# Forgetting attention with a SiLU MoE on one core: transposes of two batches moved ahead, and MoE pieces spread evenly between the steps

## The chip, the core and the metric

The kernel runs on one core of a Trainium2 chip. The metric is the device time of one execution in microseconds, taken as the median over several runs. The five engines are written as in the profile: PE is TensorE (matmuls; PEld are its weight loads), ACT is ScalarE, DVE is VectorE, POOL is GpSimd, and SP is the queue from which most transfers are started.

## The reference

Attention with a forget gate over 8 batches of 8 heads, 576 rows and head width 64, and after it a two-layer MoE with a SiLU in between, on the 4608 rows of all batches:

```python
scores = scale * q @ k.T                     # 8 x 8 x 576 x 576
decay = cum[:, None] - cum[None, :]          # cum = cumsum(log f)
attn = softmax(where(causal, scores + decay, -1e9))
x = (attn @ v).transpose(0, 2, 1, 3).reshape(4608, 512)
h = x @ w_in                                 # 512 -> 2048
out = (h * sigmoid(h)) @ w_out               # 2048 -> 512
```

The decay is folded into the values: they, and a column of ones beside them, are multiplied by exp(-cum) (`w_bf`), so a softmax is an exponential, a mask, a matmul and a division by the last column.

## The kernel before, in words

**The attention, first blocks.** Of each batch the first 128 rows are a block that can be done alone. For one batch b there are these steps on TensorE, with their lines in the profile:

- `turn0(b)`: q and k of the block are transposed by 32 small matmuls (L271) into two tiles `tp`; q's is copied into a tile `qkT` by ACT, k's into `kT0[b]` by DVE (L278).
- `ban0(b)` (batches 0 to 3 only): two matmuls (L286) put the causal mask into a tile `sc`.
- `scores0(b)`: eight matmuls (L305) into `sc`; ACT takes the exponential into `u` (L312). For batches 4 to 7 `mask0(b)` multiplies `u` by the triangle on DVE (L321).
- `out0(b)`: eight matmuls of `u` and the values (L340) into a tile that takes a buffer of the same kind as `sc`; DVE makes the reciprocal (L348) and the product `xq` (L350).
- `back0(b, copy)`: four transposes of `xq` (L362), and a copy into the MoE's input by ACT or DVE (L364).

Batches 0 to 3 are done by an order written out by hand, before any MoE work is possible. Batches 4 and 5, then 6 and 7, are done by `two_more(b)`, with MoE work between the steps.

**The rest of the attention.** A loop over 16 values of m takes two pairs of heads per turn: `scores` (L433, exponentials L437 and L449), `attend` (L478 and L487, with L495 and L496 on DVE) and, a turn later, `back` (L508). Between them stand calls of `slot`, which fill in MoE work.

**The MoE.** The rows are in ten groups: one of 512 tokens (the blocks of batches 0 to 3), two of 256 (batches 4 and 5, batches 6 and 7), and later ones of 384 and 256. Its work is cut into pieces of four matmuls on TensorE. An m1 piece (`m1_chunk`, L532) makes one `hp` tile of the first product; ACT takes the tanh (L540) and DVE makes `gt` of it (L541). An m2 piece (`m2_part`, L570) adds a quarter of the second product into a tile `po`; after the fourth, ACT copies it out (L579) and it is stored.

**Who decides the order.** Every engine works through its queue in the order in which the program is written. `step()` writes the next piece, m1 or m2. When both can be done it compares how far each is in its group; if the two fractions are less than 0.3 apart it takes the kind that wasn't taken last, else the one that is behind. `fill(us, first)` calls `step()` until pieces worth `us` have been written, by an estimate of their length; what was written too much is kept in `at["left"]` and deducted from the next call, so a call may write no piece. `first` names the kind to begin with.

**Buffers.** PSUM is used up by two tiles of the kind `sc` (scores, and the products of `out0`) and four of the kind `big` (`tp`, `hp`, `po`, `tx`, and the products of `attend`). The tiles `qkT` have three buffers; from batch 4 on, two of them are taken by the transposed q and k of the loop's first two turns, so that the two batches of a `two_more` share the third.

Of the kernel before, what the change touches and what calls it, by code (L numbers as in the profile page):

```python
# [18 lines left out]
def kernel(  # L19
# [110 lines left out]
    def load_v0(b):  # L130
        t = vfs[b % 4]
        nc.sync.dma_start(out=t[:, :, 0:D], in_=v[b, :, 0:P, :].rearrange("h p d -> p h d"))
        vf0[b] = t
# [85 lines left out]
    def keep_warm(n):  # L219
        t = pbig.tile([P, SM], FP32, name="wm", tag="big")  # L220
        for _ in range(n):
            nc.tensor.matmul(t[:, :], lhsT=warm[:, 0:P], rhs=warm[:, :], start=True, stop=True)  # L222
# [37 lines left out]
    def turn0(b, between=0):  # L260
        src = qk0.pop(b)
        qT0[b] = qktp.tile([P, NP, P], BF16, name="qkT", tag="qkT")
        for i, (dst, evac) in enumerate(
            ((qT0[b], nc.scalar.copy), (kT0[b], nc.vector.tensor_copy))
        ):
            if i == 1 and between:
                keep_warm(between)
            tp = pbig.tile([P, NP, NRUN, RUN], FP32, name="tp", tag="big")
            for c in range(RUN):
                for j in range(2):  # L270
                    nc.tensor.matmul(  # L271
                        tp[j * D : (j + 1) * D, :, :, c].rearrange("p a r -> p (a r)"),
                        lhsT=src[:, i, c * D : (c + 1) * D],
                        rhs=sel[:, j, :],
                        start=True,
                        stop=True,
                    )
            evac(  # L278
                out=dst[:, :, :].rearrange("p a t -> p (a t)"),
                in_=tp[:, :, :, :].rearrange("p a r c -> p (a r c)"),  # L280
            )

    def ban0(b):
        sc = psc.tile([P, 2, NP, P], FP32, name="sc", tag="sc")
        for i in range(2):
            nc.tensor.matmul(  # L286
                sc[:, i, :, :].rearrange("p a t -> p (a t)"),
                lhsT=ident_bf[:, :],
                rhs=ban[:, :, :].rearrange("p a t -> p (a t)"),
                start=True,  # L290
                stop=False,
            )
        return sc

    def scores0(b, sc=None):
        t = qT0.pop(b)
        fresh = sc is None
        u = upool.tile([P, 2, NP, P], BF16, name="u", tag="u")
        u0[b] = u
        if fresh:  # L300
            sc = psc.tile([P, 2, NP, P], FP32, name="sc", tag="sc")
        for p in range(NP):
            for i in range(2):
                r = slice(i * D, (i + 1) * D)
                nc.tensor.matmul(  # L305
                    sc[:, i, p, :],
                    lhsT=kT0[b][r, p, :],
                    rhs=t[r, p, :],
                    start=fresh,
                    stop=fresh or p == NP - 1,  # L310
                )
        nc.scalar.activation(  # L312
            out=u[:, :, :, :].rearrange("p i a t -> p (i a t)"),
            in_=sc[:, :, :, :].rearrange("p i a t -> p (i a t)"),
            func=ACT.Exp,
            scale=scale,
        )

    def mask0(b):
        x = u0[b][:, :, :, :].rearrange("p i a t -> p (i a) t")  # L320
        nc.vector.tensor_tensor(  # L321
            out=x, in0=x, in1=tri[:, None, :].to_broadcast([P, H, P]), op=ALU.mult
        )
# [11 lines left out]
    def out0(b):  # L335
        dn = psc.tile([P, 2, 4, P], FP32, name="dn0", tag="sc")
        u = u0.pop(b)
        for h in range(H):
            p, i = h // 4 * 2 + h % 2, h // 2 % 2
            nc.tensor.matmul(  # L340
                dn[:, h // 4, h % 4, 0 : D + 1],
                lhsT=u[:, i, p, :],
                rhs=v0[b][:, h, :],
                start=True,
                stop=True,
            )
        rec = recp.tile([P, 2, 4], FP32, name="rec0", tag="rec0")
        nc.vector.reciprocal(out=rec[:, :, :], in_=dn[:, :, :, D])  # L348
        xq = xqp.tile([P, H, D], BF16, name="xq", tag="xq")
        nc.vector.tensor_tensor(  # L350
            out=xq[:, :, :].rearrange("p (g j) d -> p g j d", g=2),
            in0=dn[:, :, :, 0:D],
            in1=rec[:, :, :, None].to_broadcast([P, 2, 4, D]),
            op=ALU.mult,
        )
        xqs[b] = xq

    def back0(b, copy):
        xq = xqs.pop(b)[:, :, :].rearrange("p (c j) d -> p c (j d)", j=2)
        tx = pbig.tile([P, NCC, P], BF16, name="tx", tag="big")  # L360
        for cc in range(NCC):
            nc.tensor.transpose(tx[:, cc, :], xq[:, cc, :], ident_bf[:, :])  # L362
        g, c0 = HEADS_OF[b]
        copy(out=xg(g)[:, :, c0 : c0 + P], in_=tx[:, :, :])  # L364
# [160 lines left out]
    def m1_chunk(g, fc):  # L525
        w = GW[g]
        if fc == 0:
            gts[g] = gpool.tile([P, NFC, w], BF16, name="gt", tag="gt")
        gt = gts[g]
        hp = pbig.tile([P, w], FP32, name="hp", tag="big")  # L530
        for cc in range(NCC):
            nc.tensor.matmul(  # L532
                hp[:, :],
                lhsT=w_in_bf[:, cc, fc * P : (fc + 1) * P],
                rhs=xg(g)[:, cc, :],
                start=(cc == 0),
                stop=(cc == NCC - 1),
            )
        th = tpool.tile([P, w], BF16, name="th", tag="th")
        nc.scalar.activation(out=th[:, :], in_=hp[:, :], func=ACT.Tanh, scale=0.5)  # L540
        nc.vector.scalar_tensor_tensor(  # L541
            out=gt[:, fc, :],
            in0=th[:, :],
            scalar=1.0,
            in1=hp[:, :],
            op0=ALU.add,
            op1=ALU.mult,
        )
# [43 lines left out]
        else:  # L592
            M2 += [(g, tb, part) for tb in range(nt) for part in range(4)]
    M2_OF = [sum(1 for x in M2 if x[0] == g) for g in range(NG)]
    at = {"m1": 0, "m2": 0, "left": 0.0, "last": 0}
    ready: set[int] = set()
    open2 = {"w": False}

    def step():

        a, c = at["m1"], at["m2"]
        can1 = a < len(M1) and M1[a][0] in ready
        g1 = M1[a][0] if a < len(M1) else NG
        g2 = M2[c][0] if c < len(M2) else NG
        if can1 and M1[a][1] == 0 and g1 > g2 + 1:
            can1 = False
        can2 = open2["w"] and c < len(M2) and g2 < g1
        if not can1 and not can2:
            return None
        if can1 and can2:  # L610
            f1 = M1[a][1] / NFC
            f2 = (c - sum(M2_OF[:g2])) / M2_OF[g2]
            can1 = at["last"] == 2 if abs(f1 - f2) < 0.3 else f1 < f2
        at["last"] = 1 if can1 else 2
        if can1:
            m1_chunk(*M1[a])
            at["m1"] += 1
            return 4 * (GW[g1] / 2.4 + 2.5)
        m2_part(*M2[c])
        at["m2"] += 1  # L620
        return 4 * (DM / 2.4 + 2.5)
# [3 lines left out]
        t += sum(4 * (DM / 2.4 + 2.5) for g, _, _ in M2[at["m2"] :] if g in ready)  # L625
        return t / 1000

    def fill(us_, first=0):
        if first:
            at["last"] = 3 - first  # L630
        at["left"] += us_ * 1000
        while at["left"] > 0:
            t = step()
            if t is None:
                at["left"] = 0.0
                return False
            at["left"] -= t
        return True


# [17 lines left out]
    turn0(1)  # L658
    sc = ban0(0)
    scores0(0, sc)  # L660
    sc = ban0(1)
    scores0(1, sc)
    convert_v0(1)
    load_w_in(1)
    load_v0(4)
    turn0(2)
    out0(0)
    sc = ban0(2)
    scores0(2, sc)
    convert_v0(2)  # L670
    load_v0(5)
    turn0(3)
    out0(1)
    back0(0, on_dve)
    sc = ban0(3)
# [49 lines left out]

    def two_more(b):
        turn0(b)
        fill(0.6)
        turn0(b + 1)
        fill(0.6)  # L730
        scores0(b)
        mask0(b)
        fill(0.6, 2)
        scores0(b + 1)
        mask0(b + 1)
        fill(2.0, 2)
        out0(b)
        fill(0.6)
        out0(b + 1)
        fill(1.2)  # L740
        back0(b, on_act)
        fill(0.6)
        back0(b + 1, on_act)
        fill(0.6)

    fill(4.0)
    two_more(4)
    ready.add(1)
    fill(6.0)
    open2["w"] = True  # L750
    fill(5.0, 2)
    two_more(6)
    ready.add(2)
    fill(1.0, 2)
# [56 lines left out]
    while step() is not None:  # L811
        pass
# [31 lines left out]
```

The softmax here doesn't subtract the row's maximum and nothing guards it: scores larger than these inputs give would overflow.

## Time and profile before

| what | value |
|---|---|
| time, median of 3 runs | 355.41 us (355.34 to 355.89) |
| span of the profiled run | 353.1 us |
| TensorE, VectorE, ScalarE, GpSimd busy | 341.9, 188.0, 218.1, 103.4 us |
| first m1 piece starts | 19.84 us |
| first blocks of batches 4 and 5 | 24.2 to 36.4 us |
| first blocks of batches 6 and 7 | 48.5 to 60.2 us |
| the loop over m starts | 62.0 us |
| last `back` ends, MoE alone from there | 291 us |

Times within the profile are counted from the start of the span. In the timelines below each line has the start, the length, engine, source line, operation, output and input tiles, their sizes and how many instructions were joined; in brackets stands how long the engine was idle just before and what it waited for. Matmuls overlap each other and their ends are modelled, so what a group of them costs TensorE is read from its start to the start of the next group.

### The profile page before, as it was taken

Reading aid. Unit: us, or ns where it says so; the run is one execution under the profiler, and the core shown is the slowest. Engines: PE = TensorE matmul, PEld = TensorE weight load, DVE = VectorE, ACT = ScalarE, POOL = GpSimd, SP = SyncE. Lnnn points to the kernel's source line nnn. Section 1 sums busy time; section 2 is a strip of 40 time slices with the busy share of each in tenths; the row PEclk is TensorE's granted clock in tenths of the full one; section 3 lists DMA queues with packets and bytes.
Section 4 is the critical chain, followed back from the end, with each engine's and each line's share of the span. In section 5 each row is a group of like instructions: output and inputs, shape, how many; then the busy total and the mean of one; then the engine's idle time right before and its main releaser. Section 6 shows DMA issues by size and latency. Waiting matters only on the chain.

```text
span 353.1 us, 9039 instructions
## 1 busy us (share of the span) xinstructions
PE 341.9 (97%) x3646; PEld 205.0 (58%) x3646; DVE 188.0 (53%) x409; ACT 218.1 (62%) x399; POOL 103.4 (29%) x183
## 2 busy tenths in 40 slices
PE   8998999999899999999999999999999999999995
PEld 4644555667656556566565666656566565555664
DVE  4566834355657466555646654645655554535340
ACT  5646716866676756758758675676946744545341
POOL 6993146254072162145117214312600000000000
PEclk9999999999999999999999999999999999999999
DMA  8999998998885895696489594748822000010012
GB/s 161 221 203 200 200 196 177 214 220 171 191 167 126 178 183 97 147 212 151 113 174 211 116 201 106 174 103 165 170 58 58 32 32 30 30 59 33 32 60 59
DMA packets 138969, 47.92 MB, mean 136 GB/s; under 512 B 127984, under 2 KB 134384, under 8 KB 138928
## 3 DMA queue, kind: packets, MB, share of 16 engines
q1 hardware_dynamic: 132240, 40.93, 53.5%
q0 software_dynamic: 6528, 6.29, 10.8%
q8 instruction: 28, 0.46, 0.6%
q10 hardware_dynamic: 160, 0.13, 0.1%
q14 instruction: 13, 0.11, 0.1%
HBM read 36.85 MB, written 9.44 MB: 131 GB/s over the span
## 4 chain that ended last, share of the span: by engine, by line
PE 88%; ACT 4%; DVE 4%; issue 2%; ACTq 0%
PE po L570 35%; PE hp L532 32%; PE sc L433 7%; PE dn L478 5%; PE dn L487 3%; PE tp L271 2%; PE tx L508 2%; DVE gt L541 2%; PE wm L222 1%; DVE xq L350 1%; ACT th L540 1%; ACT u L437 1%; ACT osb L579 1%; ACT u L312 1%; ACT qkT L278 1%
## 5 line engine op out<-in xcount | busy, mean ns | idle before, releaser
L532 PE MATMUL hp<-x,w_in_bf 128*128 128x384 bf16 (+2 forms) x832 | 148.4, 314 | 3.3 <-DVE gt L541 2.3
L540 ACT ACTIVATE th<-hp 128x384 bf16<-128x384 f32 (+2 forms) x208 | 95.7, 475 | 88.8 <-PE hp L532 86.4
L541 DVE SCALAR_TENSOR_TENSOR gt<-th,hp 128x384 bf16<-128x384 bf16 (+2 forms) x208 | 106.1, 522 | 82.8 <-ACT th L540 79.4
L570 PE MATMUL po<-w_out_bf,gt 128*128 128x512 bf16 (+1 forms) x592 | 145.7, 374 | 0.0
L532 PEld LDWEIGHTS <-w_in_bf 128*128 128x128 bf16 x832 | 78.1, 98 | 58.5 <-issue 5.5
L570 PEld LDWEIGHTS <-gt 128*128 128x128 bf16 x592 | 55.4, 98 | 49.1 <-issue 1.7
L437 ACT ACTIVATE u<-sc 128x1024 bf16<-128x1024 f32 (+1 forms) x96 | 74.6, 814 | 12.1 <-PE sc L433 11.9
L387 POOL TENSOR_TENSOR vp<-vf,w_bf 128x520 bf16<-128x520 f32 (+1 forms) x32 | 35.7, 1118 | 44.9 <-DMA vf<-in_v_dram 42.8
L442 DVE TENSOR_TENSOR u<-u,tri 128x768 bf16<-128x768 bf16 x32 | 21.2, 663 | 21.7 <-ACT u L437 21.7
L373 POOL CAST qkb<-qf 128x384 bf16<-128x384 f32 x32 | 16.5, 516 | 54.4 <-DMA qf<-in_q_dram 53.5
L579 ACT ACTIVATE osb<-po 128x512 f32<-128x512 f32 (+1 forms) x37 | 21.9, 592 | 15.4 <-PE po L570 15.4
L433 PE MATMUL sc<-qkT 64*128 64x128 bf16 (+1 forms) x640 | 26.6, 207 | 0.1
L456 DVE TENSOR_TENSOR ut<-ut,trit 128x128 bf16<-128x128 bf16 x32 | 8.1, 252 | 31.3 <-ACT ut L449 31.1
L433 PEld LDWEIGHTS <-qkT 64*128 64x128 bf16 x640 | 18.3, 94 | 8.6 <-issue 6.0
L449 ACT ACTIVATE ut<-sc 128x640 bf16<-128x640 f32 x32 | 22.8, 711 | 0.0
L478 PEld LDWEIGHTS <-u 128*128 128x128 bf16 x576 | 20.7, 97 | 2.5
L478 PE MATMUL dn<-vp,u 128*128 128x65 bf16 x384 | 21.8, 193 | 0.0
L373 POOL CAST qkb<-kf 128x384 bf16<-128x384 f32 x32 | 16.3, 509 | 15.5 <-DMA kf<-in_k_dram 15.5
L496 DVE TENSOR_TENSOR xr<-dn,rec 128x448 bf16<-128x448 f32 x32 | 20.0, 624 | 1.1
L478 PE MATMUL dn<-v,u 128*128 128x65 bf16 x192 | 19.8, 193 | 0.0
L377 POOL CAST qkb<-qktf 128x128 bf16<-128x128 f32 x32 | 10.2, 318 | 20.1 <-DMA qktf<-in_k_dram 20.1
L433 PE MATMUL sc<-qkT,kT 64*128 64x64 bf16 (+1 forms) x128 | 16.0, 258 | 0.0
(64 smaller groups left out, 193.2 us busy)
## 6 DMA issues: line engine op xcount, KB each, us to landing
vf<-in_v_dram SPq DMA_DIRECT2D x32, 256.0 KB, 5.1
out_dram<-osb SPq DMA_DIRECT2D x32, 256.0 KB, 2.3
qf<-in_q_dram SPq DMA_DIRECT2D x64, 96.0 KB, 2.8
kf<-in_k_dram SPq DMA_DIRECT2D x64, 96.0 KB, 2.7
w_in_bf<-in_moe_w_in_dram POOLq DMA_DIRECT2D x4, 512.0 KB, 9.1
w_out_bf<-in_moe_w_out_dram POOLq DMA_DIRECT2D x4, 512.0 KB, 12.9
qkb<-in_q_dram POOLq DMA_DIRECT2D x8, 128.0 KB, 6.8
qkb<-in_k_dram POOLq DMA_DIRECT2D x8, 128.0 KB, 7.0
```

Source lines behind the costliest of these rows:

```text
L373: nc.gpsimd.tensor_copy(out=t2[:, c0 : c0 + NR, :].rearrange("p c x -> p (c x)"), in_=t[:, :, :, :].rearrange("p c h d -> p (c h d)"),)
L387: nc.gpsimd.tensor_tensor(out=vbf[b][r, c, :, :], in0=vst[b][c][r, :, :], in1=w_bf[r, c + 1, b * H : (b + 1) * H, None].to_broadcast([n, H ...
L433: nc.tensor.matmul(sc[:, i, o : o + q1 - q0], lhsT=kt, rhs=t[r, q0:q1], start=True, stop=True)
L437: nc.scalar.activation(out=u[:, :, c * SM : c * SM + w], in_=sc[:, :, 0:w], func=ACT.Exp, scale=scale)
L442: nc.vector.tensor_tensor(out=x, in0=x, in1=tri[:, None, None, :].to_broadcast([P, 2, NR, P]), op=ALU.mult,)
L449: nc.scalar.activation(out=ut[:, :, 0:3:2, :].rearrange("p k i t -> p i k t"), in_=sc[:, :, T0 : T0 + (NM + 1) * ST].rearrange("p i (k t) ...
L478: nc.tensor.matmul(dn[:, i * NR + c - 1, :], lhsT=u[:, i, o : o + P], rhs=vals(kb, i), start=(kb == 0), stop=(kb == c),)
L532: nc.tensor.matmul(hp[:, :], lhsT=w_in_bf[:, cc, fc * P : (fc + 1) * P], rhs=xg(g)[:, cc, :], start=(cc == 0), stop=(cc == NCC - 1),)
L540: nc.scalar.activation(out=th[:, :], in_=hp[:, :], func=ACT.Tanh, scale=0.5)
L541: nc.vector.scalar_tensor_tensor(out=gt[:, fc, :], in0=th[:, :], scalar=1.0, in1=hp[:, :], op0=ALU.add, op1=ALU.mult,)
L570: nc.tensor.matmul(po[:, :], lhsT=gt[:, fc, tb * P : (tb + 1) * P], rhs=w_out_bf[:, fc, m0:m1], start=(fc == 0), stop=(fc == NFC - 1),)
L579: nc.scalar.activation(out=osb[:, :], in_=po[:, :], func=ACT.Copy, scale=0.5)
```

## The change

Two things are changed. In the hand-written order, the transposes of batch 2 now stand ahead of the mask and the scores of batch 1, and those of batch 3 ahead of those of batch 2; this is for having the queries and keys of a batch copied well before its scores. In the filling, `two_more` now asks for at least one MoE piece between any two of its steps (`least`), with slightly smaller amounts in three places, and `step()` alternates more strictly: the band in which it alternates is narrower (0.15 instead of 0.3), and after two pieces of a kind in a row it takes the other kind if that can be done. `step()` serves the whole kernel, so the order of MoE pieces changes everywhere, while the pieces themselves are the same.

```diff
     def step():
         if can1 and can2:
-            can1 = at["last"] == 2 if abs(f1 - f2) < 0.3 else f1 < f2
-        at["last"] = 1 if can1 else 2
+            want = 3 - at["last"] if abs(f1 - f2) < 0.15 else (1 if f1 < f2 else 2)
+            if want == at["last"] and at["row"] >= 2:
+                want = 3 - want
+            can1 = want == 1
+        kind = 1 if can1 else 2
+        at["row"] = at["row"] + 1 if kind == at["last"] else 1
+        at["last"] = kind
...
-    def fill(us_, first=0):
+    def fill(us_, first=0, least=0):
         if first:
-            at["last"] = 3 - first
+            at["last"], at["row"] = 3 - first, 2
         at["left"] += us_ * 1000
-        while at["left"] > 0:
+        while at["left"] > 0 or least > 0:
             t = step()
...
             at["left"] -= t
+            least -= 1
...
     turn0(1)
     sc = ban0(0)
     scores0(0, sc)
+    turn0(2)
     sc = ban0(1)
     scores0(1, sc)
...
-    turn0(2)
     out0(0)
+    turn0(3)
     sc = ban0(2)
     scores0(2, sc)
...
-    turn0(3)
     out0(1)
...
     def two_more(b):
         turn0(b)
-        fill(0.6)
+        fill(0.6, 0, 1)
         turn0(b + 1)
-        fill(0.6)
+        fill(0.6, 0, 1)
         scores0(b)
         mask0(b)
-        fill(0.6, 2)
+        fill(0.6, 2, 1)
         scores0(b + 1)
         mask0(b + 1)
-        fill(2.0, 2)
+        fill(1.6, 2, 1)
         out0(b)
-        fill(0.6)
+        fill(0.6, 0, 1)
         out0(b + 1)
-        fill(1.2)
+        fill(0.8, 0, 1)
         back0(b, on_act)
-        fill(0.6)
+        fill(0.6, 0, 1)
         back0(b + 1, on_act)
-        fill(0.6)
+        fill(0.6, 2, 1)
```

More of the change, by code (lines that the diff above doesn't have):

```diff
@@ L594 @@
     M2_OF = [sum(1 for x in M2 if x[0] == g) for g in range(NG)]
-    at = {"m1": 0, "m2": 0, "left": 0.0, "last": 0}
+    at = {"m1": 0, "m2": 0, "left": 0.0, "last": 0, "row": 0}
     ready: set[int] = set()
```

## The prediction

> **What bounds the kernel now.** I read the page first, then busy time by stage, then TensorE's timeline beside those of ScalarE and VectorE around each edited stretch.
>
> ```profile
> PE 341.9 (97%) x3646; PEld 205.0 (58%) x3646; DVE 188.0 (53%) x409; ACT 218.1 (62%) x399; POOL 103.4 (29%) x183
> ...
> PE 88%; ACT 4%; DVE 4%; issue 2%; ACTq 0%
> ...
> L532 PE MATMUL hp<-x,w_in_bf 128*128 128x384 bf16 (+2 forms) x832 | 148.4, 314 | 3.3 <-DVE gt L541 2.3
> ```
>
> TensorE is the bound: 97% busy, 88% of the chain that ended last. So the change can only win or lose the time in which TensorE stands still, and busy time doesn't show that well: one L532 matmul reads 314 ns, while 384-wide ones start 163 ns apart (0.65 us for a piece of four). I therefore count from start to start. A piece of the first MoE product (m1, four matmuls) takes 0.87, 0.65 or 0.44 us for 512, 384 or 256 tokens, one of the second (m2) 0.87. What goes beyond that is standstill: about 2.4 us between 24.2 and 47.5 (the blocks of batches 4 and 5), 1.7 between 47.5 and 60.2 (batches 6 and 7), 1.7 from 60 to 100, 1.7 from 100 to 290, nothing after.
>
> The first blocks, TensorE's timeline and then ScalarE's:
>
> ```profile
> 11.41 1.08 PE L271 MATMUL tp<-sel,qkb 128*64 128x64 bf16 x32
> 12.43 0.43 PE L340 MATMUL dn<-v,u 128*128 128x65 bf16 x8
> 12.70 0.59 PE L286 MATMUL sc<-ban,ident_bf 128*128 128x512 bf16 x2
> 13.29 0.40 PE L305 MATMUL sc<-qkT,kT 64*128 64x128 bf16 x8
> 13.61 1.08 PE L271 MATMUL tp<-sel,qkb 128*64 128x64 bf16 x32
> ...
> 15.12 0.59 PE L286 MATMUL sc<-ban,ident_bf 128*128 128x512 bf16 x2
> 15.65 0.40 PE L305 MATMUL sc<-qkT,kT 64*128 64x128 bf16 x8
> 16.42 0.42 PE L340 MATMUL dn<-v,u 128*128 128x65 bf16 x8 [0.37 <-DVE xq L350]
> ...
> 17.33 0.42 PE L340 MATMUL dn<-v,u 128*128 128x65 bf16 x8
> ...
> 19.84 0.38 PE L532 MATMUL hp<-x,w_in_bf 128*128 128x512 bf16 x1 [0.67 <-ACT x L364]
> ```
> ```profile
> 13.72 1.02 ACT L312 ACTIVATE u<-sc 128x1024 bf16<-128x1024 f32 x1 [0.65 <-PE sc L305]
> 14.64 0.58 ACT L278 CAST qkT<-tp 128x512 bf16<-128x512 f32 x1
> 16.09 1.02 ACT L312 ACTIVATE u<-sc 128x1024 bf16<-128x1024 f32 x1 [0.86 <-PE sc L305]
> ```
>
> Until 15.98 TensorE waits for almost nothing; then the exponential of batch 3 (16.09) sets 17.33 and all up to the first m1 at 19.84. An exponential starts 0.44 us after its scores start, takes 1.02, and ends 0.22 before what reads it.
>
> Later, TensorE's timeline of batches 4 and 5, and of two runs of m1 pieces:
>
> ```profile
> 28.50 0.40 PE L305 MATMUL sc<-qkT,kT 64*128 64x128 bf16 x8
> 29.63 0.40 PE L305 MATMUL sc<-qkT,kT 64*128 64x128 bf16 x8 [0.73 <-ACT qkT L278]
> ```
> ```profile
> 222.87 1.92 PE L532 MATMUL hp<-x,w_in_bf 128*128 128x256 bf16 x16
> 225.62 0.60 PE L532 MATMUL hp<-x,w_in_bf 128*128 128x256 bf16 x4 [0.83 <-DVE gt L541]
> ```
>
> Batch 5's queries wait for the third qkT buffer until batch 4's scores have read it. The fifth 256-piece in a row finds all four "big" buffers waiting for tanh and gt, which queue behind four exponentials.
>
> **What the skill says.** "Perfetto Trace Analysis", section Identifying the Most-Contended Engine: matmul busy time misleads, since matmuls are pipelined; the 314 against 163 ns agree. "PSUM — Partial Sum Buffer", Specifications: eight banks of 2 KiB per partition. The kernel's two "sc" tiles of two banks and four "big" tiles fill all eight, which is why both lines above end on a buffer. "Trainium Architecture — The Big Picture", Inside one NeuronCore: each engine has its own instruction stream, tied to others by semaphores alone. So an instruction placed early and not ready holds up what follows it on its own engine; the waits above agree.
>
> **Part 1, transposes of batches 2 and 3 moved ahead.** Nothing is added. I replay the changed program's order from 10.54, the end of batch 0's scores, with before's steps from start to start (transposes T of a batch 1.02, ban 0.53, scores 0.33, out 0.27, back 0.22): T2 10.54 to 11.56 (its loads landed at 10.2 and 11.0), ban and scores of 1 to 12.42, out 0 to 12.69, T3 to 13.71 (landed 11.9 and 12.8), ban 2 to 14.24, scores 2 to 14.57, out 1 and back 0 to 15.06. Exponential 1 runs 12.53 to 13.55, in time for ban 2, which takes its buffer. Exponential 2 now starts at 14.24+0.44=14.68 instead of 13.72, for T3 stands before its scores, and ends at 15.70; ban 3 needs that buffer and waits from 15.06 to 15.81. Scores 3 then start at 16.34 instead of 15.65, and exponential 3, out 3 and the first m1 follow at the same distances. That wait is new: behind it on TensorE stand the whole remainder of the blocks and all MoE work. **+0.69**, m1 at 20.53. T5 waited for loads that land at 26.3 and 26.9, so it gives 0.27 back: **-0.27**. If exponential 2 hid completely the part would cost 0; if the later copies stretched it too, 0.9. I take 0.69.
>
> **Part 2, at least one piece between steps (4 and 5).** Between the two scores stands now an m1 of 0.87, which hides the 0.73 qkT wait. But only one piece stands between scores 5 and out 4, three before. Scores 4 start at 28.82; ScalarE does the qkT copy (29.31), tanh, exponential 4 (30.28 to 31.30), tanh, exponential 5 (31.70 to 32.72). The masks (0.69 on VectorE) end at 32.04 and 33.46. TensorE is ready for out 4 at 31.32 and waits to 32.09; out 5, ready at 33.23, waits to 33.51; the two back transposes wait 0.3 each for xq behind gt pieces. The thirteenth m1 starts at 36.62 against 36.41, with equal work done: 0.21 late, where 0.42 came in. **-0.21**.
>
> **The same for batches 6 and 7.** Two of four "big" buffers hold open m2 sums. From 36.62 before's 6.76 us for eleven m1 pieces, less one of 0.44, lead to 42.94; five m2 (4.33), two m1 (0.87) and 0.1 (which every piece ahead of transposes or scores takes longer) start T6 at 48.24. m2 between T6 and T7 hides T6's copies, whose 0.29, 0.12 and 0.52 of standstill go. But an m1 stands right after T7 and takes the buffer of T7's keys: it waits for transposes (51.23), 0.11, and a 0.69 copy: 0.85 lost. Then exponential 6 is behind qkT7 and a tanh: 53.94 to 54.96, mask to 55.70; out 6, ready at 55.12, waits 0.63, out 7 0.69. Batch 7's back ends at 60.02 with two 256-pieces (0.88) less done than before at 60.19: 0.71 late. **+0.50**.
>
> **Part 3, no three alike in a row, and the 0.15 band.** step() decides for the whole kernel, so orders shift everywhere; the number of matmuls doesn't. m = 0: standstill at its scores falls from 0.38 to 0.14 (another m2 stands before the last scores). **-0.21**. m = 1: none, the 0.21 at its last scores stays. m = 2: six 256-pieces in a row become five; no m2 is left, and the fifth waits about as long (1.09 against 1.12): none. From 100 on, before loses 1.00 at 222.87 (3.18 us for five pieces of 0.437), twice 0.29 (246.91 and 276.65, four 384-pieces in 2.90 instead of 2.61) and twice 0.07, 1.72 in all. In the changed order the longest run there is three. For the worst of these, three 256-pieces ahead of an attend, I find 0.15: the attend takes the buffer of an output copy that ends 2.80 after the last scores started, the pieces end at 2.70. With one 0.07 left and 0.03 for rounding, 0.25 remains. Pairs of 384 ahead of an attend stood already in before (239.59: 1.29 for two, attend in its usual 1.71), at no cost. **-1.47**. After 290 neither order has standstill.
>
> Sum: 0.69-0.27-0.21+0.50-0.21-1.47 = -0.97; 355.41-0.97 = 354.4.
>
> **Rivals.** (a) The long runs are gone, but their standstill returns in front of attends and back transposes, since ScalarE's queue is the same; with 1.0 of the 1.47 kept as loss: 355.4, no change. For it: the five-piece run of m = 2 loses as much as six did. Against: from 100 on ScalarE is idle 31% (130.9 busy of 189.9), and runs of three cost nothing there in before. (b) Part 1 and the m1 behind T7 are hidden better than my replay has it, and only the gains stay: no 0.69 and so no 0.27, and 0.50-0.85 = -0.35; 355.41-0.21-0.35-0.21-1.47 = about 353.2. For it: the first blocks' exponentials are ScalarE's only long work there. Against: both waits follow from which buffer the changed program gives to whom. (c) Slower: the pairs cost 0.1 ahead of each of 14 attends and a third of the gain goes: +0.69-0.27-0.21+0.50-0.21 = +0.50 before 100, +1.4-0.98 after: +0.9, 356.3. For it: the one attend replayed at 0.15. Against: the row at 239.59.
>
> **How the numbers follow.** Forecast 0.57, (a) 0.25, (b) 0.08, (c) 0.10. The first three lie between 353.2 and 355.4; the unknown of each replay is some 0.3, four replays together 0.6, so 353.5 to 355.7 leaves out most of (c), of (b), and the forecast's tail. Faster by over 0.2% is below 354.70: most of the forecast and all of (b), 0.60. Slower is above 356.12: 0.08. The rest, 0.32, is the same.
>
> **What would show it.** First m1 at 20.5, with a wait of some 0.7 us before batch 3's ban; qkT no longer ahead of scores 5; a wait of about 0.8 for kT's copy on the m1 after T7; waits for u at out 4, 6 and 7; from 100 to 290 one standstill of 0.15 in place of 1.72. The first m1 at 19.8 or earlier, or standstill in front of most attends, would prove me wrong.

## The result, and the profile after

The changed kernel takes 354.39 us (median of 6 runs, 354.12 to 355.05) against 355.47 (355.34 to 355.89): a ratio of 0.9971, 95% interval 0.9958 to 0.9984. It is faster by 1.1 us, and by 0.6 to 1.5 within the interval.

The three lines of the page of the changed kernel that answer to those shown of before:

```profile
PE 336.8 (96%) x3598; PEld 203.7 (58%) x3646; DVE 188.8 (54%) x409; ACT 218.3 (62%) x399; POOL 103.2 (29%) x183
...
PE 89%; ACT 3%; DVE 2%; issue 2%; DMA 2%; POOL 1%; POOLq 0%; ACTq 0%
...
L532 PE MATMUL hp<-x,w_in_bf 128*128 128x384 bf16 (+2 forms) x829 | 145.9, 314 | 2.6 <-DVE gt L541 0.8
```

TensorE's share of the chain rose by a point, and the idle time ahead of L532 that ends on gt fell from 2.3 to 0.8. The busy time says nothing here: 48 matmul records are missing (3598 of 3646), so 341.9 and 336.8 are not to be compared. DMA is new in the chain, with 2%: it is the load of batch 2's keys, which shows in the next timeline.

TensorE's timeline of the first blocks in the changed kernel, then ScalarE's exponentials of batches 2 and 3 (start and duration in us, operation, in brackets the idle time before it and what ended it):

```profile
10.40 0.64 PE L271 MATMUL tp<-sel,qkb 128*64 128x64 bf16 x16
11.21 0.64 PE L271 MATMUL tp<-sel,qkb 128*64 128x64 bf16 x16 [0.17 <-DMA qkb<-in_k_dram]
...
13.01 1.08 PE L271 MATMUL tp<-sel,qkb 128*64 128x64 bf16 x32
...
16.08 0.59 PE L286 MATMUL sc<-ban,ident_bf 128*128 128x512 bf16 x2 [0.53 <-ACT u L312]
16.60 0.40 PE L305 MATMUL sc<-qkT,kT 64*128 64x128 bf16 x8
...
20.65 0.59 PE L532 MATMUL hp<-x,w_in_bf 128*128 128x512 bf16 x2 [0.67 <-ACT x L364]
```
```profile
15.00 1.02 ACT L312 ACTIVATE u<-sc 128x1024 bf16<-128x1024 f32 x1 [0.67 <-PE sc L305]
17.04 1.02 ACT L312 ACTIVATE u<-sc 128x1024 bf16<-128x1024 f32 x1 [1.01 <-PE sc L305]
```

Exponential 2 starts at 15.00 in place of 13.72 (14.68 was forecast), and the ban of batch 3 waits for it, as worked out: from the `back` ahead of it to the ban's start TensorE loses 0.68. New to the working is the second line: the transposes of batch 2 now start so early that their half of the keys waits for its load, which puts exponential 2 some 0.3 later than forecast.

TensorE's timeline of the changed kernel in the blocks of batches 4 and 5, and 6 and 7:

```profile
29.03 0.40 PE L305 MATMUL sc<-qkT,kT 64*128 64x128 bf16 x8
29.36 0.82 PE L532 MATMUL hp<-x,w_in_bf 128*128 128x512 bf16 x3
30.33 0.40 PE L305 MATMUL sc<-qkT,kT 64*128 64x128 bf16 x8
...
32.31 0.43 PE L340 MATMUL dn<-v,u 128*128 128x65 bf16 x8 [0.61 <-DVE u L321]
...
52.29 0.60 PE L532 MATMUL hp<-x,w_in_bf 128*128 128x256 bf16 x4 [0.79 <-DVE kT L278]
...
55.89 0.43 PE L340 MATMUL dn<-v,u 128*128 128x65 bf16 x8 [0.40 <-DVE u L321]
...
57.29 0.43 PE L340 MATMUL dn<-v,u 128*128 128x65 bf16 x8 [0.54 <-DVE u L321]
```

The line with x3 is a piece of four with one record missing. The 0.73 ahead of scores 5 is gone; out 4, the m1 after the transposes of batch 7, and outs 6 and 7 wait instead.

The stretch that held a run of five 256-wide pieces (222.87 in the kernel before) is now this, in the changed kernel:

```profile
223.12 1.04 PE L570 MATMUL po<-w_out_bf,gt 128*128 128x512 bf16 x4
224.00 1.47 PE L532 MATMUL hp<-x,w_in_bf 128*128 128x256 bf16 x12
225.47 0.19 PE L478 MATMUL dn<-v,u 128*128 128x65 bf16 x1
```

An m2 stands behind the scores, and three pieces take 1.47 instead of 1.31: 0.16 of standstill in place of 1.00. Counted from start to start, standstill from 100 to 290 us falls from 1.77 to 0.35. (The three m1 stand in a row in spite of the rule because no m2 could be done there; more on this under "Pieces between the steps alone".)

### The profile page after: what moved, and what is told of

The parts are those of the page before. It is cut to its first block, busy times and chain, and to the rows that moved or that the text cites. A ratio compares the mean times of both kernels' runs of the same rounds, so it can differ in the third digit from the quotient of the medians.

```text
span 352.4 us, 8990 instructions
## 1 busy us (share of the span) xinstructions
PE 336.8 (96%) x3598; PEld 203.7 (58%) x3646; DVE 188.8 (54%) x409; ACT 218.3 (62%) x399; POOL 103.2 (29%) x183
## 4 chain that ended last, share of the span: by engine, by line
PE 89%; ACT 3%; DVE 2%; issue 2%; DMA 2%; POOL 1%; POOLq 0%; ACTq 0%
PE po L570 35%; PE hp L532 34%; PE sc L433 7%; PE dn L478 5%; PE dn L487 3%; PE tx L508 2%; DMA qkb<-in_k_dram 2%; PE tp L271 2%; ACT u L312 1%; DVE gt L541 1%; ACT u L437 1%; POOL qkb L124 1%; DVE xq L350 1%; ACT th L540 1%; PE sc L305 1%
## 5 line engine op out<-in xcount | busy, mean ns | idle before, releaser
L532 PE MATMUL hp<-x,w_in_bf 128*128 128x384 bf16 (+2 forms) x829 | 145.9, 314 | 2.6 <-DVE gt L541 0.8
L570 PE MATMUL po<-w_out_bf,gt 128*128 128x512 bf16 (+1 forms) x550 | 139.3, 374 | 3.2 <-issue 1.6
L532 PEld LDWEIGHTS <-w_in_bf 128*128 128x128 bf16 x832 | 78.9, 98 | 56.6 <-issue 3.2
L570 PEld LDWEIGHTS <-gt 128*128 128x128 bf16 x592 | 54.2, 98 | 48.7 <-issue 2.5
L387 POOL TENSOR_TENSOR vp<-vf,w_bf 128x520 bf16<-128x520 f32 (+1 forms) x32 | 34.0, 1063 | 45.3 <-DMA vf<-in_v_dram 43.0
L456 DVE TENSOR_TENSOR ut<-ut,trit 128x128 bf16<-128x128 bf16 x32 | 9.3, 291 | 33.3 <-ACT ut L449 33.3
```

Source lines behind the costliest of these rows:

```text
L387: nc.gpsimd.tensor_tensor(out=vbf[b][r, c, :, :], in0=vst[b][c][r, :, :], in1=w_bf[r, c + 1, b * H : (b + 1) * H, None].to_broadcast([n, H ...
L532: nc.tensor.matmul(hp[:, :], lhsT=w_in_bf[:, cc, fc * P : (fc + 1) * P], rhs=xg(g)[:, cc, :], start=(cc == 0), stop=(cc == NCC - 1),)
L570: nc.tensor.matmul(po[:, :], lhsT=gt[:, fc, tb * P : (tb + 1) * P], rhs=w_out_bf[:, fc, m0:m1], start=(fc == 0), stop=(fc == NFC - 1),)
```

## The experiments

In the table below, "T5 done" is the start of the first piece behind the transposes of batch 5, in the profiled execution; "rest" is the span less that; spans are given to 0.1 us, so a rest is good to about 0.05. Every time is about 1.8 us longer than its span, in every execution. The kernel before ran again beside each group; its medians were 355.49, 355.54 and 355.49.

```
kernel                        time (range), us           ratio to before [95%]     T5 done  rest
before                        355.47 (355.34-355.89)                                27.53  325.57
changed                       354.39 (354.12-355.05)  0.9971 [0.9958, 0.9984]       28.06  324.34
x1 part 1 undone              354.24 (353.93-354.26)  0.9958 [0.9945, 0.9971]       28.17  324.33
x2 part 1 alone               355.56 (355.27-356.19)  1.0001 [0.9993, 1.0010]       28.79  325.51
x3 step() alone               354.95 (354.46-355.81)  0.9983 [0.9975, 0.9991]       28.28  325.72
x3b the same again            355.05 (354.33-355.77)  0.9985 [0.9976, 0.9995]       28.37  325.63
x4 pieces in steps alone      354.62 (354.23-355.05)  0.9974 [0.9963, 0.9984]       27.65  324.85
b1 before again               356.27 (one run)                                      28.89  325.61
y4 m2 behind T7               354.68 (354.40-354.72)  0.9972 [0.9962, 0.9983]       28.22  324.68
s1 part 1 undone, early load  353.59 (353.37-353.88)  0.9948 [0.9935, 0.9962]       27.34  324.76
s2 changed, early load        354.21 (354.05-354.77)  0.9968 [0.9956, 0.9981]       28.10  324.30
c1 band without the rule      354.71 (354.01-355.67)  0.9980 [0.9972, 0.9988]       28.08  324.52
x5 counted pieces             353.44 (353.42-353.53)  0.9941 [0.9929, 0.9954]       27.67  324.03
best: x5, early load, no rule 354.04 (353.82-354.44)  0.9964 [0.9951, 0.9976]       27.32  324.88
```

**Part 1, undone and alone.** The edit, forward for x2 (on the kernel before), backward for x1 (on the changed one):

```diff
     scores0(0, sc)
+    turn0(2)
     sc = ban0(1)
...
-    turn0(2)
     out0(0)
+    turn0(3)
     sc = ban0(2)
...
-    turn0(3)
     out0(1)
```

> The changed kernel with its first blocks put back in the old order (turn0(2) after convert_v0(1), turn0(3) after the scores of batch 2). Theory: part 1 costs time, because the ban of batch 3 waits for a later exponential 2. The first m1 then starts at about 19.84 us again instead of 20.65, the transposes of batch 5 wait 0.27 for their load again, and the kernel takes about 353.9 us, 0.5 less than the changed one. Rival 1: the loss of part 1 is taken up entirely further on, by waits that are there anyway: 354.4. Rival 2: moving the transposes is what won the time: about 354.9 or more.

> The kernel before with only the two turn0 calls moved. Theory: about +0.5 us (+0.81 at the first m1, -0.27 for the load wait of batch 5's transposes): 355.9 us, first m1 near 20.65. Rival: the move wins or hides: 355.5 or less, with the first m1 near 19.8 or its delay gone by the thirteenth m1 piece.

Without part 1 the first m1 starts at 19.99, with it alone at 20.72: the delay is there. But it hardly reaches the end: 354.24 against 354.39, and 1.0001 for part 1 alone. Both theories (353.9 and 355.9) miss, and the rivals by which the delay is taken up further on are nearer. TensorE's timeline in x1 (part 1 undone), and the line of its chain of waits (start, duration, what) that ends on that wait:

```profile
25.41 1.04 PE L532 MATMUL hp<-x,w_in_bf 128*128 128x512 bf16 x4
26.94 1.29 PE L271 MATMUL tp<-sel,qkb 128*64 128x64 bf16 x32 [0.49 <-DMA qkb<-in_q_dram]
28.17 1.04 PE L532 MATMUL hp<-x,w_in_bf 128*128 128x512 bf16 x4
```
```profile
17.23 9.66 DMA qkb<-in_q_dram
26.90 0.04 issue
```

The chain no longer comes from the blocks of batches 0 to 3 but from the load of batch 5's queries, on its way for 9.66 us. The m1 ahead takes 1.53 from start to start instead of 0.97, the transposes 1.23 instead of 1.02: 0.77 of waiting, where the profile of before had shown 0.27. A delay on TensorE before this point is taken up by that wait. In x2 the load even comes last with part 1 in place: its transposes start at 27.57, after 0.39 of waiting.

**The kernel before again.** The same kernel, profiled a second time.

> The kernel before, unchanged, for a second profile. Theory: executions differ up to the transposes of batch 5, because these wait for batch 5's query load, and are alike after it. In the profiles so far this load let the transposes start at 26.31 (before), 26.42, 26.94, 27.06 and 27.57 us in the other kernels with the old fills or the old head. So the start here is anywhere from 26.3 to 27.8, the scores of batch 0 start anywhere from 10.0 to 11.0, and from the end of those transposes to the end of the program it takes 325.5 to 325.6 us again, as in the first profile (27.53 to 353.1). Rival: executions differ later too; then that distance is off by 0.3 or more.

The same rows in this second execution of the kernel before:

```profile
27.64 1.33 PE L271 MATMUL tp<-sel,qkb 128*64 128x64 bf16 x32 [0.30 <-DMA qkb<-in_q_dram]
28.89 0.39 PE L532 MATMUL hp<-x,w_in_bf 128*128 128x512 bf16 x1
```

It took 356.27 us, 1.41 more than the execution profiled first (354.86). 1.36 of that lies ahead of this point, and the rest is 325.61 against 325.57. That is as expected. So the first profile showed an execution whose early loads came soon; most of before's times (354.78 to 356.47 over all groups) are longer.

**The load moved forward.** On x1 (s1) and on the changed kernel (s2):

```diff
     load_qk0(4)
-    load_w_in(2)
     load_qk0(5)
+    load_w_in(2)
     load_w_in(3)
```

> The changed kernel with the old first blocks, and batch 5's load issued ahead of the third piece of w_in in place of behind it. Theory: that load is what the transposes of batch 5 wait for, in every kernel with the old first blocks (0.3 to 1.0 us in the profiles); it now lands some 2 us earlier, the wait goes, and the time falls from 354.24 to between 353.4 and 353.9. Rival: the loads ahead of it are the limit, it lands no earlier: 354.2.

> The changed kernel, with batch 5's load issued ahead of the third piece of w_in. Theory: the changed kernel hardly waited for that load (its TensorE comes later), so there is little to gain: 354.1 to 354.4, and part 1's full delay of about 0.8 us at the first m1 now stands in the time, as the difference to the same kernel with the old first blocks (0.5 to 0.9). Rival: part 1 costs no more than the 0.15 that the two medians differ by with the late load: 353.6 to 353.9 here.

Both as expected: 353.59 and 354.21. In s1 the load, now issued at 16.49, lands after 7.6 us, and TensorE no longer waits:

```profile
25.36 1.04 PE L532 MATMUL hp<-x,w_in_bf 128*128 128x512 bf16 x4
26.32 1.08 PE L271 MATMUL tp<-sel,qkb 128*64 128x64 bf16 x32
27.34 1.04 PE L532 MATMUL hp<-x,w_in_bf 128*128 128x512 bf16 x3
```

The two differ by part 1 alone, and now by 0.62: its price when that load doesn't hide it. (In their profiles T5 is done 0.76 later with part 1; s1 loses part of its lead again further on, see the last section.) With the late load it was 0.15. This pair shows both halves: the load is what hid part 1, and part 1 by itself is a loss.

**step() alone, twice.** The kernel before with the changed step() (and the row that fill sets for it) and nothing else; its core:

```diff
-            can1 = at["last"] == 2 if abs(f1 - f2) < 0.3 else f1 < f2
+            want = 3 - at["last"] if abs(f1 - f2) < 0.15 else (1 if f1 < f2 else 2)
+            if want == at["last"] and at["row"] >= 2:
+                want = 3 - want
```

> The kernel before with only step() changed (no three alike in a row, alternation within 0.15), old first blocks, old fills in two_more. Theory: nearly all of the change's gain is here: the long runs of 256- and 384-wide m1 pieces after 100 us go, 1.3 to 1.5 us come back: about 354.0 us, standstill from 100 to 290 us near 0.35 instead of 1.72. Rival (a): the standstill returns ahead of the attends: 355.4. Rival (b): the gain was in the pieces between the steps, not in step(): 355 or more.

> Part 3 alone once more, unchanged, because its profile (355.81 us) lay at the top of its 22 times (median 354.95). Theory: from the end of batch 5's transposes to the end it takes 325.7 us again, 0.15 more than before, so that the whole difference between its executions is ahead of that point; the median is within 0.4 of that of before. Rival: the stretch after it is shorter than in the first profile, 325.2 or less, and part 3 alone does win about 0.5.

The time, 354.95, misses the 354.0 of the theory and lies next to rival (b), 355 or more. From 100 to 290 us the standstill is 0.48, nearly as low as in the changed kernel. Yet the rest is 325.6 to 325.7, no shorter than before, in both profiles: with the old fills, too, the new step() puts an m1 behind the transposes of batch 7, which waits 0.79 for kT's copy, and the second of the two outs then waits for its mask 1.12. TensorE's timeline in x3:

```profile
53.06 0.60 PE L532 MATMUL hp<-x,w_in_bf 128*128 128x256 bf16 x4 [0.79 <-DVE kT L278]
...
57.39 0.42 PE L340 MATMUL dn<-v,u 128*128 128x65 bf16 x8
58.94 0.43 PE L340 MATMUL dn<-v,u 128*128 128x65 bf16 x8 [1.12 <-DVE u L321]
```

Between 47.5 and 100 us it stands still for 4.9 where before does for 3.4, which is what it wins after 100 and a little more. The medians are 0.5 below before, though; both profiled executions were at the top of their ranges (355.81 and 355.77). The theory for the profile holds, the one for the median doesn't. An estimate says that the shorter executions were shorter in the rest too: with the earliest first m1 of any profile (19.70 in x5), the 7.41 from there to T5 done that s1 takes without a wait, the rest of 325.65 and the 1.8, the time would be 354.56, and 8 of the 34 times lie below that. What they did otherwise was not seen, so this stays open.

**Pieces between the steps alone.** The kernel before with the changed fills of two_more and fill()'s least; the first of eight lines (two amounts shrink, 2.0 to 1.6 and 1.2 to 0.8, and the last line asks for an m2 first):

```diff
         turn0(b)
-        fill(0.6)
+        fill(0.6, 0, 1)
...
```

> The kernel before with only the new fill amounts and the least of one piece in two_more, old first blocks, old step(). Theory: the 0.73 wait for qkT goes, out 4 and out 5 wait instead; the later blocks lose again; together between -0.2 and +0.4, and the orders of the later pieces shift a little (one run of four 256-pieces is left, about 0.5 of standstill): 354.6 to 355.4 us. Rival: the pieces between the steps are the gain: 354.3 or less.

0.9 faster, at the good end of what was expected, and the rest is 0.72 shorter. It is not the blocks themselves that give this: from 47.5 to 60 it loses 1.96 against 1.69. It is that the standstill from 100 to 290 fell to 0.61 with the old step(): another amount of work done by 60 us shifts every order behind it, and all but one of the long runs (0.45 at 223.33) go. TensorE's timeline in x4 at that place:

```profile
222.45 1.04 PE L570 MATMUL po<-w_out_bf,gt 128*128 128x512 bf16 x4
223.33 2.07 PE L532 MATMUL hp<-x,w_in_bf 128*128 128x256 bf16 x16
225.53 0.19 PE L478 MATMUL dn<-v,u 128*128 128x65 bf16 x1
```

Following step() through the program shows why such runs depend on all that was written earlier. An m2 can be written only for a group whose m1 are all written. When the m2 in hand run out, the m1 left of the current group stand in a row, whatever the band or the rule says. At this place five m1 are left in the kernel before, four in x4, three in the changed kernel. So the two edits share one gain; 0.72 here and about -0.1 in x3 don't add to the 1.23 of both.

**The narrow band without the rule of two.** On x1:

```diff
-            if want == at["last"] and at["row"] >= 2:
-                want = 3 - want
```

> The changed kernel with the old first blocks and without the rule of no three in a row: only the narrower band (0.15) is left of step()'s edit. In this order no run of m1 pieces is longer than three between two steps from the scores of m = 0 on. Theory: the band is what breaks the long runs, and the rule even makes the run of five at m = 2: its 1.0 goes too, from 100 to 290 us the standstill stays under 0.6, and the time is 353.1 to 353.8. Rival: the rule of two is needed, without it standstill comes back ahead of scores and attends: 354.5 or more.

A miss. The run of five at m = 2 does go (two pieces and 0.42 at 86.88 are left), but from 100 to 290 us the standstill is 0.99 instead of 0.35, and the time is 354.71, as the rival had it. (Of the 0.47 over x1 the two profiles show only 0.1; c1's was one of its shorter executions, 354.36.) The rule does work that the length of runs doesn't show. The last kernel shows it best.

**An m2 behind the transposes of batch 7.** On the changed kernel:

```diff
         turn0(b + 1)
-        fill(0.6, 0, 1)
+        fill(0.6, 2, 1)
```

> The changed kernel with the piece behind the transposes of batch 7 asked to be an m2 (first=2 in that fill), so that no m1 needs the buffer of batch 7's keys there. Theory: the 0.79 wait of that m1 for the copy of kT goes, no later wait takes it up in full: 353.6 to 354.0 us, from 354.39. Rival: the exponential of batch 6 is then the limit and outs 6 and 7 wait longer by the same amount: 354.3 or more.

The rival is right: 354.68. TensorE's timeline in y4:

```profile
55.85 0.43 PE L340 MATMUL dn<-v,u 128*128 128x65 bf16 x8 [0.61 <-DVE u L321]
...
57.25 0.43 PE L340 MATMUL dn<-v,u 128*128 128x65 bf16 x8 [0.54 <-DVE u L321]
...
63.92 0.40 PE L433 MATMUL sc<-qkT 64*128 64x128 bf16 x8 [0.54 <-ACT u L437]
```

The 0.79 for kT's copy is gone, out 6 waits 0.61 instead of 0.40, batch 7's back is done 0.22 earlier for the same work, and a score of m = 0 then waits 0.54 for an exponential. The waits that are left end on ScalarE and VectorE, so the wait moved on to them.

**Counted pieces.** On x1, in two_more, where pieces(n, kind) calls step() n times:

```diff
         turn0(b)
-        fill(0.6, 0, 1)
+        pieces(1)
         turn0(b + 1)
-        fill(0.6, 0, 1)
+        pieces(1, 2)
         scores0(b)
         mask0(b)
-        fill(0.6, 2, 1)
+        pieces(1, 2)
         scores0(b + 1)
         mask0(b + 1)
-        fill(1.6, 2, 1)
+        pieces(3, 2)
         out0(b)
-        fill(0.6, 0, 1)
+        pieces(1)
         out0(b + 1)
-        fill(0.8, 0, 1)
+        pieces(2)
         back0(b, on_act)
-        fill(0.6, 0, 1)
+        pieces(1)
```

> The changed step(), the old first blocks, and in the later blocks a fixed number of pieces in place of an amount of time: one after each transposes and after the first scores, three after the second scores, one and two around the outs, one between the backs, m2 where there are any. Theory: what was lost in the changed kernel at outs 4 and 5 (about 1.3) and at the m1 after the transposes of batch 7 and at outs 6 and 7 (about 1.8) goes, with some 0.5 to 1.0 given back in longer runs of m1 further on: 352 to 353 us, faster than both kernels. Rival: ScalarE and VectorE are the limit there and the waits come back elsewhere: 354 or more.

353.44, faster than both kernels, though it misses the 352 to 353 that was expected by 0.4. TensorE's timeline in x5:

```profile
29.94 0.40 PE L305 MATMUL sc<-qkT,kT 64*128 64x128 bf16 x8
30.27 2.76 PE L532 MATMUL hp<-x,w_in_bf 128*128 128x512 bf16 x12
32.87 0.42 PE L340 MATMUL dn<-v,u 128*128 128x65 bf16 x8
33.13 1.02 PE L532 MATMUL hp<-x,w_in_bf 128*128 128x512 bf16 x4
33.99 0.42 PE L340 MATMUL dn<-v,u 128*128 128x65 bf16 x8
```

Three pieces behind the second scores cover the exponentials and masks, and outs 4 and 5 wait for nothing. From 47.5 to 60 the standstill is 0.57 instead of 2.13. Of that the rest keeps only 0.3 against x1, because other places stand still: a score of m = 0 waits (0.94 at 66.37), four 384-wide pieces at 108.69 cost 0.55 and four 256-wide ones at 222.41 cost 1.00. At the last two no m2 could be done, so the m1 stand in a row. That is the shift of the orders, this time to the bad.

**All together.** x5 with the early load and without the rule of two.

> Counted pieces in the later blocks, batch 5's load issued ahead of the third piece of w_in, old first blocks, the narrow band without the rule of two. Theory: the gains add up, less two runs of four 384-wide pieces ahead of attends (about 0.5 each): from 353.44 by 0.4 for the load and by 0.5 to 1.0 for fewer long runs: 351.9 to 352.6. Rival: one of them takes the other's gain: 353.2 or more.

A miss: 354.04, slower than x5. The load gave its part (T5 done at 27.32), but the rest is 0.85 longer. Most of this lies between 60 and 100 us, where TensorE stands still for 3.3 against 2.2 in x5; from 100 to 290 it is 2.3 against 1.9. One of the places that lose, TensorE's timeline in this kernel, then at the same place in the changed one (each from a piece behind the scores to the attend's first matmul):

```profile
120.47 2.12 PE L532 MATMUL hp<-x,w_in_bf 128*128 128x384 bf16 x12
123.30 0.19 PE L478 MATMUL dn<-v,u 128*128 128x65 bf16 x1 [0.70 <-DVE gt L541]
```
```profile
121.66 1.04 PE L570 MATMUL po<-w_out_bf,gt 128*128 128x512 bf16 x4
122.54 1.46 PE L532 MATMUL hp<-x,w_in_bf 128*128 128x384 bf16 x8
123.84 0.19 PE L478 MATMUL dn<-v,u 128*128 128x65 bf16 x1
```

Three m1 directly behind the scores: their tanh and gt queue behind the exponentials, and the attend waits 0.70. With an m2 first there is no wait. In the changed step() the slot's first=2 sets row to 2, so that the rule forces that m2; without the rule, a difference of progress above 0.15 puts an m1 there. Following step() through the program bears this out: both kinds could be done here, and m1 was behind by 0.42, 0.35 and 0.29. Four m1 behind the scores at 92.51 (0.87 lost) come about in the same way, and so do the two m1 behind the scores at 223.03 in c1 (0.40 lost). The rule was not put back into this kernel by itself, so how much of the 0.85 is due to it is not shown.

## Why the prediction was right

The forecast was 354.4, the time is 354.39, and the sum -0.97 stands against -1.08 measured. The steps are less exact than the sum, and that the two times agree to 0.01 is luck: part 1 was put some 0.3 too dear, and parts 2 and 3 together 0.16 too good.

- **Part 1** (+0.69, -0.27). The wait for exponential 2 and its size are right: first m1 at 20.65 for 20.53, after batch 2's keys had waited for their load, which the working had without a wait; 0.62 in the times once T5's load doesn't hide it. The term that was mis-sized is T5's load: the 0.27 came from one execution, and in the other profiles that waited there it was 0.4 to 1.2. So part 1 costs about 0.1 (0.15 between x1 and the changed kernel, 0.07 alone), not 0.42.
- **Batches 4 and 5** (-0.21). The scores' 0.73 went, and the waits came where forecast: from start to start 0.78 at out 4, 0.27 at out 5, 0.3 at each back. From T5 done to the thirteenth m1 it takes 8.76 against 8.88: -0.12.
- **Batches 6 and 7** (+0.50). All three waits are there (0.79, 0.40, 0.54). From the thirteenth m1 to batch 7's back it takes 23.35 against 23.78 with two 256-pieces (0.87) less done: +0.44.
- **Part 3** (m = 0: -0.21, after 100: -1.47). From 60 to 100 us 1.52 for 1.75, from 100 to 290 0.35 for 1.77: -0.23 and -1.42, and the one place predicted at 0.15 shows 0.16. The sums are right, but within the first the places are not: the scores of m = 0 still lose 0.28 (0.14 forecast, 0.39 before), and the run at m = 2, put at no gain, wins 0.12. And the name is not right: these are gains of the changed order, and the pieces between the steps alone bring most of them (0.61 left), while step() alone gives them back in the blocks.
- **Rival (a)**, standstill back ahead of attends, didn't happen in the changed kernel, but in c1 and in the last kernel. **Rival (b)** had part 1 hidden, which holds for the time (the load hides it) but not for the first m1, and the m1 behind T7 was not hidden. **Rival (c)** put 0.98 of standstill back after 100 us; 0.35 is all that is there.

Parts 2 and 3 together were put at -1.39; the rest is shorter by 1.23.

Two readings of the working don't hold, though no term rests on them. That the tiles of PSUM fill all its banks can be why the run at 222.87 ends on a buffer, but not why scores 5 did: the third `qkT` buffer isn't in PSUM. And the page of the Trainium skill that it cites, "Perfetto Trace Analysis" (Identifying the Most-Contended Engine), has pipelined matmuls look smaller in a trace, while 314 ns for a spacing of 163 is larger; the two agree only in that busy time misleads.

## What to carry to other kernels

Profile the kernel twice before taking a wait for a load from one trace: split the span at the last such wait, and see on which side executions differ. Where a hand-written order is filled by a planner, credit a gain to the order that comes out and not to the line that was edited, since any change of the amounts shifts every order behind it. And ask what stands directly behind an instruction that loads a slower engine: here a piece that doesn't need that engine did better there, and run length alone didn't tell.

## What the runs showed of the hardware that was not expected

Executions of one unchanged kernel ranged from 354.78 to 356.47 us, and the profiles of 354.86 and 356.27 differ by 1.36 us up to the last early load and by 0.04 in the 325.6 us after it. A 128 KB load issued at 17.23 behind a 512 KB one was on its way for 9.66 us; issued in front of it, at 16.49, it landed after 7.6 us and was no longer waited for. The rest is not wholly fixed, though: s1 and x1 have the same order behind T5, and s1, 0.83 earlier there, lost 0.43 of it again, most of it in the run of five at m = 2 (3.56 for 3.29); why is not known.
